# A fused retention and hard-swish kernel: one group of attention work per block instead of two

## The chip, the cores and the metric

The kernel runs on one core of one Trainium2 chip. The metric is the device time of one execution in microseconds; the time before is the median of three runs. A profile of one further execution shows what each engine did: TensorE (PE, its weight loads PEld), VectorE (DVE), ScalarE (ACT), GpSimd (POOL) and SyncE (SP).

## The reference

Eight batches of eight heads with 576 positions of 64 numbers go through a retention layer; its output goes through a two-layer network with a hard swish.

```python
scores = q @ k^T / 8                       # [B, H, 576, 576]
ret = scores * gamma_h ** (i - j)          # where i >= j, else 0
x = (ret @ v), heads side by side          # [4608, 512]
h = x @ w_in                               # [4608, 2048]
g = h * clip(h + 3, 0, 6) / 6
out = g @ w_out                            # [4608, 512]
```

## The kernel before

**Pieces and blocks.** The 576 positions of a batch are cut into four pieces of 128 and a rest of 64; the rests of two batches form a piece. This makes 36 pieces. Four pieces fill one block of 512 tokens, so there are nine blocks, 0 to 8. The last block holds the rests.

**Retention of one piece.** A piece's output is the old state of its batch times its queries (`inter`, L361), plus masked scores times values (`intra`, L377). Scores are taken from transposed keys and queries: `scores` (L343) writes a PSUM tile of two banks, tag "sc", and gives back a mask that VectorE applies from PSUM; `scores_second` (L765) writes two banks, ScalarE copies them to a tile "raw", and its mask works from there. `update_mm` (L394) computes the new part of the state, `update_state` (L411) adds and scales it on VectorE, and `spread_state` (L427) copies it on ScalarE into a block-diagonal matrix for the next `inter`. The output is cast into the token block `xt` by ScalarE (`Output.cast`, L261).

**The network of one block.** The first layer, `gemm1` (L900), has 16 units of four 512-column matmuls; each unit's hard swish takes one ScalarE and one VectorE instruction (L449, L450). From block 1 on the second layer is done with seven products instead of eight, in the manner of Strassen and Winograd: four sums of quarters of the hidden block (`sum_of`, L514, on VectorE), seven `product`s of 16 matmuls each (L529), and a `gather` (L555) behind each. Product 6 reads sum 2, product 5 sum 1, product 7 sum 3, product 3 sum 4. Products 1, 6, 7, 4 accumulate in one bank "b", product 2 in "a", and 5, 3 in "c".

**Order around the change.** The order of all instructions on each engine is written out by hand. `seven_block` (L800) does the second layer of block kb, and among its products the retention of the four pieces c0 to c3 of block kb+1; it also starts the scores of the first two pieces, n0 and n1, of the block after that. For blocks 2 to 7 it goes so: sums 1 and 2 (and, ahead of and behind them, the scaling and DMA transposes of n0 and n1, `ahead`, L755), updates of states c2-4 and c3-4, products 1, 2, 6, a group for c0 and c1 (inter, intra, update, then scores of c2 and c3), sum 3, mask, sum 4, product 5, mask, products 7 and 3, a group for c2 and c3 (with the scores of n0 and n1), masks, product 4. Then comes the first layer of block kb+1, in which n2 and n3 are scaled and transposed, at units 1 and 5.

**Buffers.** PSUM has eight banks: four of tag "ph", two of "sc", one "o", one "tu". Keys ("kn") and queries with values ("qv") have six buffers each; POOL issues their loads (`load`, L106, three DMAs per full piece) in the order of the pieces, and each waits until its buffer is free: that of "kn" is free when `update_mm` has read it, that of "qv" when the scaled copy is made (`transpose_q`, L337). SP issues the DMA transposes and the stores of the outputs (`store2`, L620), in that order of the program.

Of the kernel before, what the change touches and what calls it, by code (L numbers as in the profile page):

```python
# [10 lines left out]
FP32 = mybir.dt.float32  # L11
FP16 = mybir.dt.float16
# [5 lines left out]
def kernel(  # L18
# [64 lines left out]
    def xt_of(kb):  # L83

        if kb not in xts:
            if kb == B:
                xts[kb] = big.tile([P, NCC, MBLK], FP16, name="xt_rest")
            else:
                xts[kb] = xpool.tile([P, NCC, MBLK], FP16, tag="xt", name=f"xt_{kb}")
        return xts[kb]  # L90
# [2 lines left out]
    EARLY = 4  # L93
    SEVEN = 1
    NBUF = 6

    def by_twos(b, s0):

# [6 lines left out]

    def load(c, parts="kqv"):  # L106
        if c not in loaded:
            kn = nat.tile([P, H, D], FP16, tag="kn", bufs=NBUF, name=f"kn_{c}")
            qv = nat.tile([P, 2, H, D], FP16, tag="qv", bufs=NBUF, name=f"qv_{c}")
            loaded[c] = {"kn": kn, "qv": qv, "q16": qv[:, 0]}  # L110
            if c < EARLY:
                loaded[c]["q2"] = q2_tile(c)
        to = {"k": (loaded[c]["kn"], k), "q": (loaded[c]["qv"][:, 0], q),
              "v": (loaded[c]["qv"][:, 1], v)}
        for dst, src in (to[part] for part in parts):
            for p0, b, s0, n in pieces[c][3]:
                if src is q and c < EARLY:
                    nc.gpsimd.dma_start(loaded[c]["q2"], by_twos(b, s0))
                    continue
                nc.gpsimd.dma_start(dst[p0:p0 + n],  # L120
                                    src[b, :, s0:s0 + n, :].rearrange("h s d -> s h d"))
# [6 lines left out]
    def load_wout(c0, c1):  # L128
# [9 lines left out]
    k0 = work.tile([P, H, D], FP32, tag="osb", bufs=4, name="whole_k_0")  # L138
    nc.sync.dma_start(k0, k[0, :, 0:P, :].rearrange("h s d -> s h d"))
    v0 = work.tile([P, H, D], FP32, tag="osb", bufs=4, name="whole_v_0")  # L140
    loaded[0] = {"kn": nat.tile([P, H, D], FP16, tag="kn", bufs=NBUF, name="kn_0"),
                 "q2": q2_tile(0), "v": v0}
    nc.gpsimd.dma_start(loaded[0]["q2"], by_twos(0, 0))
    zeros = const.tile([P, MBLK], FP16)
# [31 lines left out]

    nc.vector.memset(v0[:, 0, 0:1], 0.0)
    nc.sync.dma_start(v0, v[0, :, 0:P, :].rearrange("h s d -> s h d"))
    d2 = const.tile([HALF, 2 * H, HALF], FP16)
    nc.vector.tensor_tensor(  # L180
        out=d2, in0=ident16[0:HALF, None, 0:HALF].to_broadcast([HALF, 2 * H, HALF]),
        in1=g2q.rearrange("g t h -> g (t h)")[:, :, None].to_broadcast([HALF, 2 * H, HALF]),
# [58 lines left out]
    class Output:  # L241
# [16 lines left out]
        def pair(self, p, r=slice(0, P), cols=slice(0, P)):  # L258
            return self.banks[p // self.n][r, p % self.n, cols]

        def cast(self, xt, g0):  # L261
            engines = (nc.scalar.copy, nc.vector.tensor_copy)
            for i, bank in enumerate(self.banks):
                engines[i](xt[:, i * self.n:(i + 1) * self.n, g0:g0 + P], bank)  # L264

# [111 lines left out]
    def intra(c, copy_later=False, more=False):  # L377
        o, at, vs = st[c]["o"], st[c]["at"], st[c]["vs"]
        for p in range(NPAIR):
            for h2 in range(2):  # L380
                r = slice(h2 * HALF, h2 * HALF + HALF)
                nc.tensor.matmul(o.pair(p, r), vs[:, 2 * p + h2, :], at[:, h2, p, :],  # L382
                                 start=(st[c]["first"] and o.begins(p)),
                                 stop=(o.ends(p) and not more), skip_group_check=True)
        kb, g0 = place_of(c)

        def copy():
            o.cast(xt_of(kb), g0)

        if copy_later:  # L390
            return copy
        copy()

    def update_mm(cs):  # L394

        cs = [c for c in cs if pieces[c][0] != "rest"]
        if not cs:
            return
        u = psum.tile([P, len(cs), NPAIR, D], FP32, tag="tu", name=f"u_{cs[0]}")
        for j, c in enumerate(cs):  # L400
            kn, vs = loaded[c]["kn"], st[c]["vs"]
            st[c]["u"] = u[:, j]
            for p in range(NPAIR):
                for h2 in range(2):
                    r = slice(h2 * HALF, h2 * HALF + HALF)
                    nc.tensor.matmul(u[r, j, p, :], kn[:, 2 * p + h2, :], vs[:, 2 * p + h2, :],  # L406
                                     start=(j == 0 and p == 0),
                                     stop=(j == len(cs) - 1 and p == NPAIR - 1),
                                     skip_group_check=True)

    def update_state(c):  # L411
        kind, b, i, _ = pieces[c]
        if kind == "rest":
            return
        u = st[c]["u"]
        scale = gc_b[1 if i == PER - 1 and b % 2 else 0]
        tag, bufs = ("tf", B) if i == PER - 1 else ("ts", 2 * GROUP)
        ts = work.tile([P, NPAIR, D], FP16, tag=tag, bufs=bufs, name=f"ts_{c}")
        if i == 0:
            nc.vector.tensor_tensor(out=ts, in0=u, in1=scale, op=ALU.mult)  # L420
        else:
            ta = work.tile([P, NPAIR, D], FP32, tag="ta", bufs=2, name=f"ta_{c}")
            nc.vector.tensor_tensor(out=ta, in0=u, in1=state_of[b], op=ALU.add)
            nc.vector.tensor_tensor(out=ts, in0=ta, in1=scale, op=ALU.mult)
        state_of[b] = ts

    def spread_state(c, copy=nc.scalar.copy):  # L427

        kind, b, i, _ = pieces[c]
        if kind == "rest" or i == PER - 1:  # L430
            return
        ts, bd = state_of[b], spare.pop(0)
        spare.append(bd)
        st.setdefault(c + GROUP, {})["before"] = bd
        copy(bd[0:HALF, :, 0:D], ts[0:HALF])
        copy(bd[HALF:P, :, D:2 * D], ts[HALF:P])
# [273 lines left out]
    def load_until(c):  # L710
        while next_load[0] < NP and next_load[0] <= c:
            load(next_load[0])
            next_load[0] += 1
# [41 lines left out]
    def ahead(c):  # L755
        transpose_k(c)
        transpose_q(c)

    def load_behind(c, c1):

        turn = work.tile([P, 1], FP16, tag="turn", bufs=1, name="turn")
        nc.gpsimd.tensor_copy(turn, st[c]["vs"][:, 0, 0:1])
        load_until(c1)
# [36 lines left out]
    def seven_block(kb, mine, next_):  # L800

        seven[kb] = {}
        c0, c1, c2, c3 = mine
        n0, n1, n2, n3 = next_ or [None] * 4

        def both(which):
            for tt in range(2):
                product(kb, which, tt)

        def begin(one, other, tags):  # L810
            masks[one] = scores(one, given=True)
            masks[other] = scores_second(other, tags)

        def mask(c):
            masks.pop(c)()

        def done(*cs):
            for c in cs:
                loaded.pop(c)

        run_later(9)
        if kb > SEVEN and next_:
            ahead(n0)
        for i, q1 in done_to[kb].items():
            sum_of(kb, i, q1, 8)
        if kb == SEVEN:
            begin(c0, c1, ("ph", "ph"))
        else:
            if next_:
                ahead(n1)  # L830
            update_state(c2 - GROUP)
            update_state(c3 - GROUP)
        both(1)
        gather(kb, 1)
        spread_state((c2 if kb == SEVEN else c0) - GROUP)
        if kb == SEVEN:
            mask(c0)
            mask(c1)
            ahead(n0)
        both(2)  # L840
        gather(kb, 2)
        spread_state((c3 if kb == SEVEN else c1) - GROUP)
        if kb == SEVEN:
            sum_of(kb, 3, 0, 8)
            ahead(n1)
            load_behind(n1, c1 + NBUF)
        both(6)
        gather(kb, 6)
        if kb == SEVEN:
            both(5)  # L850
            gather(kb, 5)
            sum_of(kb, 4, 0, 8)
        inter(c0, "ph" if kb == SEVEN else "o")
        inter(c1, "ph")
        intra(c0)
        intra(c1)
        update_mm([c0, c1])
        begin(c2, c3, ("ph", "ph"))
        done(c0, c1)
        load_until(c3 + NBUF)  # L860
        if kb == SEVEN:
            mask(c2)
        else:
            sum_of(kb, 3, 0, 8)
            mask(c2)
            sum_of(kb, 4, 0, 8)
            both(5)
            gather(kb, 5)
        mask(c3)
        update_state(c0)  # L870
        if kb > SEVEN:
            spread_state(c2 - GROUP)
        both(7)
        gather(kb, 7)
        update_state(c1)
        if kb > SEVEN:
            spread_state(c3 - GROUP)
        both(3)
        gather(kb, 3)
        inter(c2, "ph")  # L880
        inter(c3, "ph")
        intra(c2)
        intra(c3)
        update_mm([c2, c3])
        done(c2, c3)
        if next_:
            begin(n0, n1, ("ph", "o"))
            load_until(n1 + NBUF)
            mask(n0)
            mask(n1)  # L890
        both(4)
        gather(kb, 4)

# [104 lines left out]
```

## Time and profile before

| What | us |
|---|---|
| median of three runs (lowest, highest) | 292.73 (292.62, 293.09) |
| the profiled execution's own time | 292.64 |
| its span, first to last instruction | 290.9 |
| block 5: product 1 to the end of product 4 | 184.86 to 200.98, 16.1 |
| block 5: first layer of block 6 behind it | 200.98 to 214.80, 13.8 |
| VectorE busy in the span | 236.8 |

Times inside the profile count from the span's start. A line of a timeline has start, length, engine, line, operation, tiles and shapes. In the chain of what ended last, a piece's length ends where its last matmul ends, while the matmuls themselves overlap: each is issued before the one ahead has left the array. A tile's name stands left of the arrow, what it is made from right of it. "DMA to landing" is the time from issue to the last byte.

### The profile page before, as it was taken

Reading aid. Unit: us, or ns where it says so; the run is one execution under the profiler, and the core shown is the slowest. Engines: PE = TensorE matmul, PEld = TensorE weight load, DVE = VectorE, ACT = ScalarE, POOL = GpSimd, SP = SyncE. Lnnn points to the kernel's source line nnn. Section 1 sums busy time; section 2 is a strip of 40 time slices with the busy share of each in tenths; the row PEclk is TensorE's granted clock in tenths of the full one; section 3 lists DMA queues with packets and bytes.
Section 4 is the critical chain, followed back from the end, with each engine's and each line's share of the span. In section 5 each row is a group of like instructions: output and inputs, shape, how many; then the busy total and the mean of one; then the engine's idle time right before and its main releaser. Section 6 shows DMA issues by size and latency. Waiting matters only on the chain.

```text
span 290.9 us, 6752 instructions
## 1 busy us (share of the span) xinstructions
PE 283.9 (98%) x2708; PEld 185.5 (64%) x2708; DVE 236.8 (81%) x410; ACT 181.4 (62%) x312; POOL 107.1 (37%) x134
## 2 busy tenths in 40 slices
PE   7999999999999999999999999999999999999993
PEld 3554456548854786478647864687468745874582
DVE  7689659999979996998699859995999599818951
ACT  6568436785477657744786668765876586437711
POOL 8953669510870077007700770067443200000000
PEclk9999999999999999999999999999999999999999
DMA  9999999999999499919992999199989960021014
GB/s 132 165 202 201 191 156 215 170 151 107 102 201 172 71 101 223 151 30 98 209 163 44 85 205 169 39 84 194 183 58 94 129 130 3 2 78 70 1 38 108
DMA packets 151807, 35.83 MB, mean 123 GB/s; under 512 B 141536, under 2 KB 147680, under 8 KB 151776
## 3 DMA queue, kind: packets, MB, share of 16 engines
q0 software_dynamic: 113664, 18.10, 89.2%
q1 hardware_dynamic: 37808, 17.05, 30.8%
q8 instruction: 21, 0.34, 0.6%
q10 hardware_dynamic: 304, 0.26, 0.3%
q14 instruction: 10, 0.08, 0.1%
HBM read 36.70 MB, written 9.44 MB: 159 GB/s over the span
## 4 chain that ended last, share of the span: by engine, by line
PE 94%; DMA 2%; DVE 1%; issue 1%; ACTq 0%; ACT 0%; POOL 0%; POOLq 0%
PE ph L442 41%; PE b L551 19%; PE c L551 10%; PE pout L492 5%; PE a L551 5%; PE o L382 4%; PE sc L350 2%; PE o L270 2%; PE ph L465 2%; DMA kn<-in_k_dram 2%; PE u L406 1%; PE sc L773 1%; PE warm L222 1%; DVE at L354 1%; PE trk L304 1%
## 5 line engine op out<-in xcount | busy, mean ns | idle before, releaser
L449 ACT ACTIVATE u<-ph,cb 128x512 f32<-128x512 f32 x144 | 98.6, 690 | 25.3 <-PE ph L442 23.0
L450 DVE SCALAR_TENSOR_TENSOR gt<-u,ph 128x512 f16<-128x512 f32 x144 | 95.8, 685 | 20.9 <-ACT u L449 18.6
L442 PE MATMUL ph<-xt,win 128*128 128x512 f16 x488 | 106.6, 379 | 0.0
L442 PEld LDWEIGHTS <-win 128*128 128x128 f16 x552 | 54.0, 98 | 63.2
L120 POOL DMA_DIRECT2D kn<-in_k_dram x39 | 33.3, 858 | 94.5 <-PE u L406 76.4
L551 PEld LDWEIGHTS <-s 128*128 128x128 f16 x512 | 49.4, 98 | 6.6 <-DVE s L525 0.2
L551 PEld LDWEIGHTS <-gt 128*128 128x128 f16 x384 | 36.3, 98 | 7.4 <-DVE gt L450 1.1
L120 POOL DMA_DIRECT2D qv<-in_v_dram x39 | 33.8, 874 | 2.8 <-DMA wout<-in_moe_w_out_dram 1.7
L120 POOL DMA_DIRECT2D qv<-in_q_dram x36 | 30.8, 862 | 5.3 <-DMA wout<-in_moe_w_out_dram 3.3
L354 DVE TENSOR_TENSOR at<-sc,mask_wide 128x1024 f16<-128x1024 f32 x19 | 23.2, 1223 | 9.5 <-PE sc L350 9.5
L551 PE MATMUL b<-tw,s 128*128 128x256 f16 x256 | 30.6, 273 | 0.0
L264 ACT CAST xt<-o 128x512 f16<-128x512 f32 (+1 forms) x32 | 17.2, 577 | 19.2 <-PE o L382 17.2
L525 DVE TENSOR_TENSOR s<-gt 128x512 f16<-128x512 f16 (+1 forms) x37 | 22.7, 614 | 0.1
L561 ACT COPY part<-b 128x512 f32<-128x512 f32 x14 | 8.2, 587 | 20.1 <-PE b L551 20.1
L340 DVE TENSOR_TENSOR vs<-qv,gqv 128x1024 f16<-128x1024 f16 x28 | 19.2, 685 | 0.0
L551 PE MATMUL b<-wout,gt 128*128 128x256 f16 x128 | 15.7, 273 | 0.0
L551 PE MATMUL b<-tw,gt 128*128 128x256 f16 x128 | 15.4, 273 | 0.0
L551 PE MATMUL c<-tw,s 128*128 128x256 f16 x128 | 15.3, 273 | 0.0
L551 PE MATMUL a<-wout,gt 128*128 128x256 f16 x128 | 15.3, 273 | 0.0
L551 PE MATMUL c<-wout,s 128*128 128x256 f16 x128 | 15.3, 272 | 0.0
L779 ACT CAST raw<-sc 128x512 f16<-128x512 f32 x28 | 15.1, 594 | 0.0
L492 PE MATMUL pout<-wout,gt 128*128 128x512 f16 x64 | 14.8, 379 | 0.0
(97 smaller groups left out, 276.6 us busy)
## 6 DMA issues: line engine op xcount, KB each, us to landing
kn<-in_k_dram POOLq DMA_DIRECT2D x31, 128.0 KB, 5.7
qv<-in_v_dram POOLq DMA_DIRECT2D x31, 128.0 KB, 6.7
qv<-in_q_dram POOLq DMA_DIRECT2D x28, 128.0 KB, 6.2
out_dram<-olo SPq DMA_DIRECT2D x7, 512.0 KB, 4.8
out_dram<-ohi SPq DMA_DIRECT2D x7, 512.0 KB, 4.9
wout<-in_moe_w_out_dram POOLq DMA_DIRECT2D x4, 512.0 KB, 14.8
win<-in_moe_w_in_dram POOLq DMA_DIRECT2D x4, 256.0 KB, 7.0
win<-in_moe_w_in_dram POOLq DMA_DIRECT2D x2, 512.0 KB, 10.6
```

The source lines that it names most:

```text
L120: nc.gpsimd.dma_start(dst[p0:p0 + n], src[b, :, s0:s0 + n, :].rearrange("h s d -> s h d"))
L264: engines[i](xt[:, i * self.n:(i + 1) * self.n, g0:g0 + P], bank)
L340: nc.vector.tensor_tensor(out=vs, in0=loaded[c]["qv"], in1=gqv, op=ALU.mult)
L354: mask = lambda: nc.vector.tensor_tensor(out=at.rearrange("t a b s -> t (a b) s"), in0=sc.rearrange("t a b s -> t (a b) s"), in1=mask_b[pi ...
L382: nc.tensor.matmul(o.pair(p, r), vs[:, 2 * p + h2, :], at[:, h2, p, :], start=(st[c]["first"] and o.begins(p)), stop=(o.ends(p) and not mo ...
L442: nc.tensor.matmul(ph, win16[:, dmc, P * fc:P * fc + P], xt_of(kb)[:, dmc, :], start=(dmc == 0), stop=(dmc == NCC - 1))
L449: nc.scalar.activation(u, ph, ACTF.Relu, bias=cb[:, 0:1], scale=1.0 / 6.0)
L450: nc.vector.scalar_tensor_tensor(out=gts[kb][:, fc, :], in0=u, scalar=1.0, in1=ph, op0=ALU.min, op1=ALU.mult)
L492: nc.tensor.matmul(pout, gt[:, fc, P * mc:P * mc + P], wout16[:, fc, :], start=(fc == 0), stop=(fc == NFC - 1))
L525: nc.vector.tensor_tensor(out=sm[i][:, q], in0=one, in1=other, op=op)
L551: nc.tensor.matmul(my[chain][tt], left[:, k, P * tt:P * tt + P], right[:, k, :], start=(first and (tt == 0 or apart) and k == 0), stop=(k ...
L779: nc.scalar.copy(raw[:, h2], banks[h2])
```

## The change

Block 1 keeps its order in a function of its own, `first_seven`. In blocks 2 to 7 `seven_block` now goes: sums 1 and 2 and the two state updates as before, product 1, scores of c2 and c3 with the mask of c2, spreading of c0 and c1's states, product 2, sum 3, mask of c3, product 6, sum 4, spreading of c2 and c3's states, products 5, 7, 3, and then one group: `inter` of all four pieces, `intra` of all four, updates of all four, scores of n0 and n1, the updates of states c0 and c1, the masks of n0 and n1, product 4. The outputs of the first three pieces lie in "ph" banks, that of the fourth in half of "sc", from which VectorE casts it. The updates of c2 and c3 lie in bank "o". All four loads of the later block are asked for behind the group. The keys have eight buffers; the table `d2`, used for the first four pieces' queries only, moves into a buffer that outputs use later.

```diff
+    KBUF = 8
...
-            kn = nat.tile([P, H, D], FP16, tag="kn", bufs=NBUF, name=f"kn_{c}")
+            kn = nat.tile([P, H, D], FP16, tag="kn", bufs=KBUF, name=f"kn_{c}")
...
-    d2 = const.tile([HALF, 2 * H, HALF], FP16)
+    d2 = work.tile([HALF, 2 * H, HALF], FP16, tag="osb", bufs=4, name="d2")
...
         if kb == SEVEN:
-            begin(c0, c1, ("ph", "ph"))
...
+            first_seven(kb, mine, next_, both, begin, mask, done)
+            return
+        if next_:
+            ahead(n1)
+        update_state(c2 - GROUP)
+        update_state(c3 - GROUP)
         both(1)
         gather(kb, 1)
...
+        begin(c2, c3, ("ph", "ph"))
+        mask(c2)
+        spread_state(c0 - GROUP)
+        spread_state(c1 - GROUP)
         both(2)
         gather(kb, 2)
...
+        sum_of(kb, 3, 0, 8)
+        mask(c3)
         both(6)
         gather(kb, 6)
...
+        sum_of(kb, 4, 0, 8)
+        spread_state(c2 - GROUP)
+        spread_state(c3 - GROUP)
+        both(5)
+        gather(kb, 5)
+        both(7)
+        gather(kb, 7)
+        both(3)
+        gather(kb, 3)
+        for c, tag in zip(mine, ("ph", "ph", "ph", "sc")):
+            inter(c, tag)
+        for c in mine[:3]:
+            intra(c)
+        intra(c3, copy_later=True)((nc.vector.tensor_copy,))
+        update_mm([c0, c1])
+        update_mm([c2, c3], "o")
+        done(*mine)
+        if next_:
+            begin(n0, n1, ("ph", "ph"))
+            load_until(n3 + GROUP)
+        update_state(c0)
+        update_state(c1)
+        if next_:
+            mask(n0)
+            mask(n1)
+        both(4)
+        gather(kb, 4)
```

More of the change, by code (lines that the diff above doesn't have):

```diff
@@ L140 @@
     v0 = work.tile([P, H, D], FP32, tag="osb", bufs=4, name="whole_v_0")
-    loaded[0] = {"kn": nat.tile([P, H, D], FP16, tag="kn", bufs=NBUF, name="kn_0"),
+    loaded[0] = {"kn": nat.tile([P, H, D], FP16, tag="kn", bufs=KBUF, name="kn_0"),
                  "q2": q2_tile(0), "v": v0}
@@ L259, in pair, with cast @@
             return self.banks[p // self.n][r, p % self.n, cols]
-        def cast(self, xt, g0):
-            engines = (nc.scalar.copy, nc.vector.tensor_copy)
+        def cast(self, xt, g0, engines=(nc.scalar.copy, nc.vector.tensor_copy)):
             for i, bank in enumerate(self.banks):
@@ L385, in intra, with copy @@
         kb, g0 = place_of(c)
-        def copy():
-            o.cast(xt_of(kb), g0)
+        def copy(*engines):
+            o.cast(xt_of(kb), g0, *engines)
         if copy_later:
@@ L392, in intra, with update_mm @@
         copy()
-    def update_mm(cs):
+    def update_mm(cs, tag="tu"):
         cs = [c for c in cs if pieces[c][0] != "rest"]
@@ L398, in update_mm @@
             return
-        u = psum.tile([P, len(cs), NPAIR, D], FP32, tag="tu", name=f"u_{cs[0]}")
+        u = psum.tile([P, len(cs), NPAIR, D], FP32, tag=tag, name=f"u_{cs[0]}")
         for j, c in enumerate(cs):
@@ L826, in seven_block @@
         if kb == SEVEN:
-            begin(c0, c1, ("ph", "ph"))
[L828 to L832, printed above, removed]
+            first_seven(kb, mine, next_, both, begin, mask, done)
[4 more added lines that the diff above has]
+        update_state(c3 - GROUP)
         both(1)
         gather(kb, 1)
-        spread_state((c2 if kb == SEVEN else c0) - GROUP)
@@ L836, in seven_block @@
[L836 to L839, printed above, removed]
+        begin(c2, c3, ("ph", "ph"))
+        mask(c2)
+        spread_state(c0 - GROUP)
+        spread_state(c1 - GROUP)
         both(2)
         gather(kb, 2)
[L842 to L846, printed above, removed]
+        sum_of(kb, 3, 0, 8)
+        mask(c3)
         both(6)
         gather(kb, 6)
[L849 to L852, printed above, removed]
@@ L853, in seven_block @@
-        inter(c0, "ph" if kb == SEVEN else "o")
+        sum_of(kb, 4, 0, 8)
[14 more added lines that the diff above has]
+        update_mm([c2, c3], "o")
@@ new lines, in seven_block, with first_seven @@
+        done(*mine)
[9 more added lines that the diff above has]
+        gather(kb, 4)
+    def first_seven(kb, mine, next_, both, begin, mask, done):
+        c0, c1, c2, c3 = mine
+        n0, n1, n2, n3 = next_
+        begin(c0, c1, ("ph", "ph"))
+        both(1)
+        gather(kb, 1)
+        spread_state(c2 - GROUP)
+        mask(c0)
+        mask(c1)
+        ahead(n0)
+        both(2)
+        gather(kb, 2)
+        spread_state(c3 - GROUP)
+        sum_of(kb, 3, 0, 8)
+        ahead(n1)
+        load_behind(n1, c1 + NBUF)
+        both(6)
+        gather(kb, 6)
+        both(5)
+        gather(kb, 5)
+        sum_of(kb, 4, 0, 8)
+        inter(c0, "ph")
@@ L860, in seven_block @@
         load_until(c3 + NBUF)
[L861 to L868, printed above, removed]
+        mask(c2)
         mask(c3)
         update_state(c0)
-        if kb > SEVEN:
-            spread_state(c2 - GROUP)
         both(7)
@@ L875, in seven_block @@
         update_state(c1)
-        if kb > SEVEN:
-            spread_state(c3 - GROUP)
         both(3)
@@ L885, in seven_block @@
         done(c2, c3)
[L886 to L890, printed above, removed]
+        begin(n0, n1, ("ph", "o"))
+        load_until(n1 + NBUF)
+        mask(n0)
+        mask(n1)
         both(4)
```

## The prediction, as it was made before the result

> **What bounds the kernel now.** I read the page first (busy shares, chain), then the table of waits, then the chain and the timelines of one block, and the DMA views last. The page's first part and the first line of its chain:
>
> ```profile
> PE 283.9 (98%) x2708; PEld 185.5 (64%) x2708; DVE 236.8 (81%) x410; ACT 181.4 (62%) x312; POOL 107.1 (37%) x134
> PE 94%; DMA 2%; DVE 1%; issue 1%; ACTq 0%; ACT 0%; POOL 0%; POOLq 0%
> ```
>
> TensorE is busy almost always and carries 94% of the chain. In the table of waits no matmul of blocks 2 to 7 stands with a wait worth naming; other engines wait for TensorE. A busy share doesn't say that the matmuls run at their pace, so I looked at the chain of block 5 (start, length, what; in us):
>
> ```profile
> 184.86 1.80 PE b L551 x16
> 186.66 1.75 PE a L551 x16
> 188.40 1.75 PE b L551 x16
> 190.15 0.45 PE o L270 x8
> 190.60 0.57 PE o L382 x16
> 191.16 0.25 PE u L406 x16
> 191.41 0.33 PE sc L350 x8
> 191.74 0.22 PE sc L773 x8
> 191.97 1.85 PE c L551 x16
> ```
>
> These are products 1, 2, 6, the first group (old state, attention, update, two scores), and product 5. A product takes 1.75 wherever it follows a product: no hole. So TensorE has nothing to win except what it loses between its own kinds of work: the product behind the scores takes 1.85, 0.10 more; the first scores take 0.33 and the second 0.22, 0.11 more; 16 attention matmuls take 0.57, where an early group of 8 takes 0.34, so 8 cost 0.23, 16 would cost 0.46, and 0.11 is the entry. **The next engine in line is VectorE**, 81% busy, and inside a block it is nearly full. Its timeline there:
>
> ```profile
> 189.28 0.42 DVE L423 TENSOR_TENSOR ta<-u,ts 128x256 f32<-128x256 f32 x1
> 189.73 0.43 DVE L424 TENSOR_TENSOR ts<-ta,gc 128x256 f16<-128x256 f32 x1
> 190.07 0.68 DVE L564 TENSOR_TENSOR olo<-part,a 128x512 f32<-128x512 f32 x1
> 190.67 1.22 DVE L525 TENSOR_TENSOR s<-gt 128x2048 f16<-128x2048 f16 x1
> 191.81 1.22 DVE L354 TENSOR_TENSOR at<-sc,mask_wide 128x1024 f16<-128x1024 f32 x1
> 192.94 1.22 DVE L525 TENSOR_TENSOR s<-gt,s 128x2048 f16<-128x2048 f16 x1
> 194.07 0.69 DVE L782 TENSOR_TENSOR at<-raw,mask_wide 128x1024 f16<-128x1024 f16 x1
> ```
>
> Each starts before the one ahead of it ends, so an instruction costs its step from start to start: 0.60 for gather 2 (L564), 1.14 for sum 3, 1.13 for the mask from PSUM, about 0.60 for the mask from SBUF. VectorE runs without a break from 184 to 196. It isn't late only because the first group keeps TensorE away from product 7 (the reader of sum 3) for 1.8 us.
>
> **The change, part by part.**
>
> *Tile shapes.* The numbers of matmuls stay. Instead of two entries into attention there is one: 0.11 saved per block. The scores of the third and fourth piece now follow a product directly, which the trace doesn't show; bounds are no entry at all (0) and twice the dearest entry (0.2). I take the 0.11 of scores behind updates, the nearest row, and the 0.10 of a product behind scores stays. Saved: 0.11 in each of six blocks, 0.66.
>
> *Scores and masks ahead of sum 3.* In the old order VectorE did gather 2, then sum 3, then the first mask. Now mask 3 (128x1024 from PSUM) stands ahead of both. VectorE comes free at 190.07, since all ahead of that (two scalings, the rest of sums 1 and 2, two state updates) is as before. Mask 190.07 to 191.20, gather 2 to 191.80, sum 3 starts 191.80 and ends 1.22 later, 193.02; a matmul starts some 0.05 after the VectorE result that it awaits: 193.07. TensorE meanwhile: the timeline starts product 2's first matmul at 186.49, 0.17 before the chain's boundary, as a matmul ends later than it issues. Behind product 1 come the entry and two scores (0.65 to product 2's start), so product 2 starts at 187.14, and products 6, 5, 7 at 188.90, 190.65 and 192.40. Product 7 waits 193.07 - 192.40 = **0.67**. Queued behind it on TensorE is everything else of the block; nothing later gives it back, since all of it is the chain. Sum 4 then ends at 194.76 (mask 4 from 192.94, 0.60; sum 4 from 193.54, 1.22) and product 3 would start at 194.82: just in time.
>
> Who pays: blocks 2, 3, 5 and 6 have the same distance from product 2's boundary to VectorE's gather 2 (3.42 us in each). Block 4 updates the states of first pieces, one instruction each instead of two:
>
> ```profile
> 158.54 0.75 DVE L420 TENSOR_TENSOR ts<-u,gc 128x256 f16<-128x256 f32 x2
> 159.21 0.68 DVE L564 TENSOR_TENSOR olo<-part,a 128x512 f32<-128x512 f32 x1
> ```
>
> There product 2's boundary is 156.72, 2.49 before VectorE's 159.21; it is 0.9 earlier, and product 7 has 0.25 to spare. Block 7 has no next block to scale for (two scalings of 0.60 less), so it doesn't wait either. Four blocks: 4 x 0.67 = 2.68.
>
> *Fourth output in the scores' bank.* The next scores need the bank out of which VectorE casts the fourth output. Between lie 32 update matmuls, 0.50. The cast starts 0.04 after the last attention matmul ends. VectorE's cast of 128x512 from PSUM isn't in the trace. Rows around it:
>
> ```profile
> L264 DVE CAST xt<-o x2: 424/424/425, 17.2 to 52.7; 128x256 f16<-128x256 f32 x2
> ```
>
> Half the size takes 0.42; the mask of twice the size 1.22; additions of 128x512 out of PSUM 0.69. I take 0.69, the same size and source. The bank is free 0.04 + 0.69 + 0.05 = 0.78 after attention's end; the scores could start 0.50 - 0.07 = 0.43 after it (0.07 is how far their first matmul starts ahead of the chain's boundary, 191.35 against 191.41). Wait **0.35**; by the ends of the cast, 0.08 to 0.88. The Trainium skill, "PSUM — Partial Sum Buffer", section on bank collisions, asks that no two engines touch one bank and quadrant at once; the trace has no such overlap. By that rule the wait can't be softened by writing another column. Blocks 2 to 6 pay, block 7 has no next scores: 5 x 0.35 = 1.75.
>
> *What stays hidden.* VectorE behind the group, from the last attention matmul's issue: cast to 0.86, two updates to 2.46, two masks to 4.20; the next first layer's first use of VectorE comes at 5.03 (scores at 1.00, product 4 at 1.55, first layer at 3.40, its first VectorE instruction 1.63 later, as 142.73 against 141.10). Spare 0.8; with that cover gone, each 0.1 costs 0.1. ScalarE's casts of outputs one to three (0.59 each) end one by one during attention, so two of the four "ph" banks are free for the second scores. Raw casts, parts (0.59 each) and eight spreading copies (0.42 each) make 6.3 us of ScalarE work beside five products and the scores, over 9 us; its last item, the copy of product 5, ends at about 193.7, and product 3 needs it at 194.8. Product 5's bank "o" is free when the second state update has read it, at 189.70; needed 190.65. The moved table for the early queries costs nothing: its buffer's next user comes after 40 us.
>
> *Loads.* POOL issues 12 loads in one run behind the group, 0.87 each, 10.4 us, instead of six and six. SP's order of transposes and stores is the old one, only the first store goes some 3 us earlier. Block 4's last transpose for the third and fourth piece landed 12.2 us after the first layer's start; it is now needed at about 15.9. Six more loads may cost up to 6 x 0.87 = 5.2, but the earlier store leaves that stretch; I count nothing. In block 1 the eight key buffers let the loads of pieces 18 and 19 go at about 85 instead of 102.7, onto a busy DMA. The last transpose for piece 15 there:
>
> ```profile
> qk<-vs SPq DMA_TRANSPOSE x1, 7.0
> ```
>
> issued at 89.45, it lands at 96.46 and is now needed at 97.94: 1.5 to spare. While loads were still landing it got through, so I take it as hidden.
>
> **Sum.** -0.66 + 2.68 + 1.75 = +3.77 on the profiled execution's 292.64 (its span of 290.9 and 1.7 around it): 296.4. The runs' median is 292.73, 0.09 above that execution; I make no correction.
>
> **Rivals.**
> *Transposes come late* (299.5). If the six added loads of block 1 are served ahead of piece 15's transpose, it lands 5.2 later, 101.7, 3.7 after its need, of which product 7's 0.67 in block 2 would have been lost anyway: +3.1. For it: DMA is full there, and a transpose alone takes a fraction of 7 us. Against: transposes land between loads in the trace. The Trainium skill, "DMA: Bandwidth & Descriptors", section on queues, rings and completion order, says that a DMA engine goes round the queues packet by packet; by it a longer load queue doesn't lengthen the turn, and the time stays that of the forecast. The trace agrees so far: a transpose issued at 85.92 landed at 94.98, ahead of a load issued at 84.61 (96.24). Chance 0.13.
> *One wait only.* VectorE half a microsecond earlier at sum 3 than I count: 292.64 + 1.75 - 0.66 = 293.7; a cast as fast as the small one: 295.0. Chance 0.12.
> *Not slower: entries between tile shapes are dearer than the rows say.* Place: the one entry less per block. Its price would have to be (2.68 + 1.75)/6 = 0.74 us to pay for both waits (292.6); from there on the change is no loss, and at 0.84 a gain of 0.6. The rows say 0.10 to 0.11. Or VectorE is late nowhere: 292.0. Together 0.10.
> Forecast 0.60; other losses, larger than these, 0.05.
>
> The range takes in the bounds of the unknown costs: 296.4 less 1.35 for the quick cast and 0.66 for no entry, 294.4, to 296.4 with 2.65 for the slow cast and 0.54 for the dear entry, 299.6; late transposes are inside. A measurement can tell about 0.2% from no change. Faster by more than that 0.05, within it 0.05, slower 0.90.
>
> **What would show it.** In the changed profile: product 7 of blocks 2, 3, 5, 6 waiting about 0.67 for VectorE's sum 3, and not in blocks 4 and 7; the scores behind the group waiting 0.35 for VectorE's cast; products at 1.75 otherwise; no matmul waiting for a transpose. I am wrong if product 7 doesn't wait, if scores of the third or fourth piece wait for a DMA, or if first-layer matmuls wait for banks.

## The result and the profile after

The changed kernel takes 296.71 us (median of four runs, 296.38 to 297.01) beside 292.68 of the kernel before (four runs, one more than in the table above): a ratio of 1.0136, 95% interval 1.0118 to 1.0154. It is slower by 4.0 us. The profiled execution took 296.49, 3.85 more than the one before, and its span grew from 290.9 to 294.7.

The first part of the page and the first line of its chain, for the changed kernel:

```profile
PE 284.1 (96%) x2708; PEld 184.9 (63%) x2708; DVE 239.2 (81%) x416; ACT 178.2 (60%) x306; POOL 107.0 (36%) x134
PE 21%; DVE 1%; ACTq 0%; ACT 0%; issue 0%
```

TensorE's busy time is what it was (283.9 before) with the same number of matmuls, so the whole difference is idle time between them. The chain's shares don't add up to the span, since it could be followed back only to 224 us; they aren't to be set against the 94% of before.

The table of waits for TensorE alone, from 90 us to the last blocks (who, for whom, us in total, times, longest):

```profile
PE sc L350 <- DVE xt L264: 1.4, 5, 0.3
PE sc L773 <- DMA qk<-vs: 1.3, 2, 0.7
PE b L551 <- DVE s L525: 1.0, 2, 0.5
```

Before, nothing stood here. Now there are three kinds of wait: scores behind the group for the cast of the fourth output (five times), scores of the fourth piece for a DMA transpose (twice), product 7 for sum 3 (twice). The second kind in TensorE's timeline, in block 2 (in brackets the idle time before the matmul and what ended it):

```profile
97.61 0.40 PE L350 MATMUL sc<-qk 64*128 64x128 f16 x8
98.69 0.40 PE L773 MATMUL sc<-qk 64*128 64x128 f16 x8 [0.69 <-DMA qk<-vs]
```

The idle time of this view begins at the modelled end of the matmul before, so it is shorter than what the start of the waiting matmul loses: 0.5 here is 0.67 of delay.

Two of the three in the chain of block 6 (start, length, what):

```profile
224.47 0.59 DVE olo L564
225.06 1.15 DVE s L525
226.21 0.04 issue
226.25 1.92 PE b L551 x16
228.17 1.75 PE c L551 x16
229.92 0.89 PE o L270 x16
230.81 1.03 PE o L382 x32
231.85 0.02 issue
231.87 0.70 DVE xt L264
232.57 0.04 issue
232.62 0.40 PE sc L350 x8
```

The chain leaves TensorE twice: for gather 2 and sum 3 on VectorE ahead of product 7 (PE b), and for the 0.70 us cast (DVE xt L264) ahead of the next scores. The updates, 0.50 us, lie beside the cast and are no longer in the chain. And VectorE's timeline in block 5:

```profile
192.39 1.22 DVE L354 TENSOR_TENSOR at<-sc,mask_wide 128x1024 f16<-128x1024 f32 x1
193.52 0.68 DVE L564 TENSOR_TENSOR olo<-part,a 128x512 f32<-128x512 f32 x1
194.11 1.22 DVE L525 TENSOR_TENSOR s<-gt 128x2048 f16<-128x2048 f16 x1
195.25 0.69 DVE L782 TENSOR_TENSOR at<-raw,mask_wide 128x1024 f16<-128x1024 f16 x1
195.86 1.22 DVE L525 TENSOR_TENSOR s<-gt,s 128x2048 f16<-128x2048 f16 x1
```

The mask now runs ahead of gather 2 and sum 3; sum 3 ends at 195.33 and product 7's first matmul starts at 195.39.

From the last first-layer matmul of a block to the first of the next, the trace gives (us):

| Block | before | after | difference | waits of TensorE there |
|---|---|---|---|---|
| 2 | 16.34 | 17.44 | +1.10 | transpose, cast |
| 3 | 15.45 | 16.48 | +1.03 | transpose, cast |
| 4 | 16.34 | 16.58 | +0.24 | cast |
| 5 | 16.34 | 17.27 | +0.93 | sum 3, cast |
| 6 | 16.34 | 17.27 | +0.93 | sum 3, cast |
| 7 | 15.64 | 15.40 | -0.24 | none |

The sum is +3.99; all else agrees within 0.2. Told by when the waiting matmuls start, the delays are 0.85 and 0.79 for the two transposes and twice 0.67 for product 7.

### The profile page after: what moved, and what is told of

It reads as the page before. It is cut to its first block, busy times and chain, and to the rows that moved or that the text cites. A ratio compares the mean times of both kernels' runs of the same rounds, so it can differ in the third digit from the quotient of the medians.

```text
span 294.7 us, 6754 instructions
## 1 busy us (share of the span) xinstructions
PE 284.1 (96%) x2708; PEld 184.9 (63%) x2708; DVE 239.2 (81%) x416; ACT 178.2 (60%) x306; POOL 107.0 (36%) x134
## 5 line engine op out<-in xcount | busy, mean ns | idle before, releaser
L450 DVE SCALAR_TENSOR_TENSOR gt<-u,ph 128x512 f16<-128x512 f32 x144 | 95.9, 683 | 16.7 <-ACT u L449 14.4
L121 POOL DMA_DIRECT2D kn<-in_k_dram x39 | 33.9, 875 | 83.0 <-PE u L406 76.8
L264 ACT CAST xt<-o 128x512 f16<-128x512 f32 (+1 forms) x27 | 14.2, 575 | 26.2 <-PE o L382 24.1
L551 PE MATMUL a<-wout,gt 128*128 128x256 f16 x128 | 15.3, 273 | 0.0
L551 PE MATMUL c<-tw,s 128*128 128x256 f16 x128 | 15.3, 273 | 0.0
L551 PE MATMUL c<-wout,s 128*128 128x256 f16 x128 | 15.3, 273 | 0.0
```

The source lines that it names most:

```text
L121: nc.gpsimd.dma_start(dst[p0:p0 + n], src[b, :, s0:s0 + n, :].rearrange("h s d -> s h d"))
L450: nc.vector.scalar_tensor_tensor(out=gts[kb][:, fc, :], in0=u, scalar=1.0, in1=ph, op0=ALU.min, op1=ALU.mult)
L551: nc.tensor.matmul(my[chain][tt], left[:, k, P * tt:P * tt + P], right[:, k, :], start=(first and (tt == 0 or apart) and k == 0), stop=(k ...
```

## The experiments

My theory: three waits, each with a cause of its own. VectorE's order makes products 7 and 3 wait; the place of the fourth output makes the next scores wait; the loads in one run make the fourth piece's transpose late, and where they do, that delay hides product 7's. The main rival: the load run slows the block as a whole, and the waits are its symptoms. The diffs are against the changed kernel, except the last. Beside the first four of these kernels the kernel before takes 292.97, beside the others 292.86, so a time is best read as its distance from that; the changed kernel's was 4.03.

### Sum 3 ahead of the masks

```diff
-        mask(c2)
         spread_state(c0 - GROUP)
...
         sum_of(kb, 3, 0, 8)
+        mask(c2)
         mask(c3)
```

> The changed kernel, with sum 3 on VectorE ahead of the masks of the third and fourth piece; sum 4 stays behind both masks. Theory A (VectorE has too much to do before products 7 and 3, whatever its order): in blocks 5 and 6 product 7 no longer waits, but sum 4 still ends when it did, so product 3 waits instead, about 0.66 us; time as the changed kernel, 296.7. Theory B (only the place of the one mask costs): the 0.67 us in blocks 5 and 6 vanish and no wait takes their place, 295.4. In both the scores behind the group wait 0.35 us in five blocks and the scores of the fourth piece wait for a transpose in blocks 2 and 3, 0.8 us each, as in the changed kernel.

Measured: 296.94, ratio 1.0135 (1.0118 to 1.0152), 3.97 above the kernel before and so as the changed kernel. The waits of TensorE in block 6:

```profile
PE c L551 <- DVE s L525: 0.5, 1, 0.5
PE sc L350 <- DVE xt L264: 0.3, 1, 0.3
```

The waiting product is now one of bank "c", product 3, and its wait is as long as product 7's was. Theory A holds: VectorE has 0.67 us too much to do ahead of the last of the two sums. Theory A named block 5 too; in this execution a late transpose took the place of that wait there (0.69 of delay), and of half of it in block 3 (0.36, with 0.31 left for product 3).

### Both sums ahead of both masks

```diff
         sum_of(kb, 3, 0, 8)
-        mask(c3)
         both(6)
         gather(kb, 6)
         sum_of(kb, 4, 0, 8)
+        mask(c2)
+        mask(c3)
```

(The mask of c2 ahead of the spreading is gone too.)

> The changed kernel, with sums 3 and 4 both ahead of the two masks. Theory A (VectorE's order around the sums is what products wait for): no product waits in blocks 5 and 6, 2 x 0.67 less, 295.4; blocks 2 and 3 keep their wait for a transpose, which had hidden this one, so nothing is gained there. Theory B (the loads in one run slow the whole block, VectorE and transposes alike): the product waits move but the time stays at 296.7.

Measured: 295.38, ratio 1.0082 (1.0067 to 1.0097), 2.41 above the kernel before. No matmul waits for a sum any more, and block 6, where no transpose is late in either kernel, is 0.24 longer than in the kernel before instead of 0.93. The rival, by which the time would stay, falls. That the expected 295.4 came out is in part luck. In the profiled execution TensorE idled for a transpose in blocks 2 (0.88) and 5 (0.45) and not in block 3: block 5, which was to gain 0.67, gained 0.07, and block 3, which was to gain nothing, gained 0.8. So which blocks pay for late transposes differs between executions. Up to the wait in block 2 this kernel, those of the experiments on sum 3, on the fourth piece and on two repairs, and the changed kernel run the same program; yet in their five executions the transpose lands 16.4 to 17.3 after the first layer's start, and TensorE loses 0.55 to 1.42 there.

### The fourth piece's attention first

```diff
+        intra(c3, copy_later=True)((nc.vector.tensor_copy,))
         for c in mine[:3]:
             intra(c)
-        intra(c3, copy_later=True)((nc.vector.tensor_copy,))
```

> The changed kernel, with the fourth piece's attention first in the group and the other three behind it, so that VectorE's cast out of the scores' bank has 0.7 us more. Theory A (the scores wait for this cast alone): the 0.35 us in blocks 2 to 6 vanish, 1.7 less, 295.0. Theory B (the wait is then taken over by the second scores, which need the banks of the first two outputs, cast later by ScalarE): a wait of up to 0.3 us stays, 296 to 296.7.

Measured: 295.72, ratio 1.0113 (1.0065 to 1.0161; one of its four runs took 298.45, so the interval is wide, and no trace shows why), 2.75 above the kernel before. No scores wait for the cast any more: block 4 goes from +0.24 to -0.07 beside the kernel before, blocks 5 and 6 from +0.93 to +0.62, so the wait was worth 0.31. Over the six blocks of the profiled execution the gain is 1.1 and not 5 x 0.31: in block 2 TensorE idled 1.25 for the transpose instead of 0.69, which ate the gain there, and in block 3 product 7's wait took the place of the transpose's. Theory B falls: the second scores wait for no cast.

### The loads spread

```diff
             ahead(n1)
+            load_behind(n1, n3)
...
-            load_until(n3 + GROUP)
+            load_until(n1 + GROUP)
...
-        load_until(n1 + NBUF)
+        load_until(n1 + GROUP)
```

The last edit is in `first_seven`; `load_behind` holds POOL back until the second piece is scaled.

> The changed kernel, with the loads spread again: two pieces behind each group, the other two behind the scaling of the second piece at the next block's start, in block 1 too. Theory A (the longer load run makes the fourth piece's transpose late in blocks 2 and 3, and this wait hides product 7's): the waits for transposes, 0.8 us each, vanish, and product 7 of blocks 2 and 3 waits 0.67 for VectorE as in blocks 5 and 6; together 0.2 less, 296.5. Theory B (the load run costs the whole difference): about 293. Theory C (the transposes are late for another reason): unchanged, with the same waits for transposes.

Measured: 296.37, ratio 1.0117 (1.0102 to 1.0132), 3.40 above the kernel before. The waits of TensorE:

```profile
PE b L551 <- DVE s L525: 2.1, 4, 0.5
PE sc L350 <- DVE xt L264: 1.4, 5, 0.3
```

The transposes are in time everywhere, and product 7 waits in four blocks instead of two: blocks 2, 3, 5 and 6 are all 0.93 longer than before. One wait had stood in front of another. This is theory A: the six blocks together are 0.25 shorter than in the changed kernel, where 0.2 was expected, and the load run costs little as long as product 7 waits anyway. The distance between the medians shrank by more, 0.6; the ratios' intervals overlap, so this difference isn't clear of noise.

### Two repairs, then three

The first kernel has the two edits of "Both sums ahead of both masks" and "The fourth piece's attention first" together:

```diff
         sum_of(kb, 4, 0, 8)
+        mask(c2)
+        mask(c3)
...
+        intra(c3, copy_later=True)((nc.vector.tensor_copy,))
         for c in mine[:3]:
             intra(c)
```

> The changed kernel, with both sums ahead of both masks and the fourth piece's attention first in its group, the loads still in one run. Theory A (three separate waits that add up): the product waits and the waits for the cast are gone, 1.35 and 1.7 less than 296.7, so 293.7; what stays is the wait for the fourth piece's transpose in blocks 2 and 3, and in some runs in block 5, 0.8 to 1.7 us in all. Theory B (the late transposes come from TensorE's other waits and go with them): 292.2.

Measured over ten runs: 293.58 (293.25 to 294.57), ratio 1.0028 (1.0017 to 1.0039). Only waits for a transpose are left in the profiled execution, 0.4 in block 2 and delays of 0.1 at most in blocks 4 and 5. With the loads spread as well:

> The changed kernel with all three repairs: both sums ahead of both masks, the fourth piece's attention first, the loads spread. Theory A: no matmul of blocks 2 to 7 waits; each of blocks 2 to 6 is 0.11 shorter than in the kernel before and block 7 is 0.24 shorter, 0.8 in all: 292.1 beside 292.9 on this chip, a ratio of 0.997. Theory B (without the waits the new order still costs something, as a further wait that the others hid): 293.5 or more.

Measured: 292.11 beside 292.86, ratio 0.9968 (0.9956 to 0.9981), faster than the kernel before by 0.3%. With product 7's wait and the cast's gone, spreading the loads is worth 1.5 us between the medians; alone it had brought little. In the trace no matmul of blocks 2 to 7 waits. Its chain in block 5, behind product 3:

```profile
196.28 0.89 PE o L270 x16
197.18 1.01 PE o L382 x32
198.19 0.50 PE u L406 x32
198.70 0.33 PE sc L350 x8
199.03 0.27 PE sc L773 x8
199.29 1.85 PE b L551 x16
```

The group runs through without a hole, and the updates are back in the chain. Blocks 2 to 6 are 0.07 to 0.08 shorter than in the kernel before, block 7 is 0.24 shorter. So without its waits the new grouping is worth 0.6 us in the blocks' lengths, 0.75 between the medians.

### The buffers alone, in the kernel before

```diff
+    KBUF = 8
...
-    d2 = const.tile([HALF, 2 * H, HALF], FP16)
+    d2 = work.tile([HALF, 2 * H, HALF], FP16, tag="osb", bufs=4, name="d2")
```

(and the eight buffers where the keys' tiles are made).

> The kernel before, with only the eight key buffers and the moved table of the change, its order of work unchanged. Theory A: no wait of TensorE comes of it; the loads of two pieces go earlier in every block and transposes land later, but scores of the third and fourth piece stand late enough: 292.9, as before. Theory B (earlier loads by themselves make transposes late enough to stop TensorE): 294 or more, with scores waiting for a transpose.

Measured: ratio 0.9999 (0.9990 to 1.0008), no block differs by more than 0.01. Yet the last transpose of piece 15 lands 16.6 us after its first layer's start, as late as in the changed kernel (16.8; in the kernel before 14.5). The late landing costs something only because the new order asks for it at 15.9. So block 2's late transpose comes from the eight key buffers, which let further loads go earlier in block 1, and not from the loads in one run, of which my theory made one cause for both blocks. In block 3 it is the run: with the buffers alone the same transpose lands at 11.8, in the changed kernel at 16.7. The experiment with spread loads undid both, since it changed block 1 too.

## Why the prediction was right, and where it was not

The forecast was 296.4, the measurement 296.7. Two of the three waits were foreseen with cause and size, the cast's in all its five blocks and product 7's in two of its four; the third, for transposes, was counted at nothing, and scores of the fourth piece waiting for a DMA stood in the prediction's own list of signs that it is wrong. By its steps:

- **VectorE ahead of product 7.** Right in place and size in blocks 5 and 6 (195.39 against a due start of 194.72: 0.67), right that block 4 is spared and that the time doesn't come back. In blocks 2 and 3 the wait didn't occur, because TensorE had already lost that time to a transpose; the run with spread loads shows that it was there behind it. "Sum 4 just in time" was right too: the chain shows product 3 following product 7 at once.
- **The cast out of the scores' bank.** Right: five times, cast 0.70 against the assumed 0.69, worth 0.31 against 0.35 (the scores do start 0.35 later, and the steps behind them give 0.03 back).
- **The entries.** Counted at 0.66, 0.11 in each of six blocks; with the waits gone they are 0.07 to 0.08 in each of five blocks and 0.24 in block 7, together 0.61. Attention took twice 0.57 in block 5 and takes 1.01, so one entry less saves 0.13; but the second scores behind the group take 0.27 where they took 0.22, and why is open. Block 7 has no such scores, and its old states, matmuls of another shape (L276), save an entry as well, twice 0.62 against 1.13. The forecast had neither the dearer second scores nor this second entry, and the totals agree by luck. That scores directly behind a product pay 0.11 was right: the first take 0.33, the second 0.22, as behind updates.
- **The loads.** This step failed, in both of its parts. For the longer run it says "I count nothing", and for block 1's earlier loads "I take it as hidden". In blocks 2 and 3 the fourth piece's scores start 0.8 us late, both times for its transpose. For block 2 the forecast kept the old landing, 96.46, with 1.5 to spare; it was 98.65. The rival that named this gave it to block 2 alone, 3.7 late. Two answers of the DMA view for the last transpose of the fourth piece in block 3's first layer, first the kernel before, then the changed one:

```profile
qk<-vs SPq DMA_TRANSPOSE x1, 3.8
```

```profile
qk<-vs SPq DMA_TRANSPOSE x1, 9.2
```

From issue to landing 3.8 and 9.2 us. Before, the loads of that stretch had landed 10.3 us after the first layer's start, and the last transposes, undisturbed, landed 0.4 to 0.6 apart. Now loads go on landing until 18.7, and transposes come 1.4 to 2.9 apart: 10.7, 13.6, 15.3, 16.7. My working asked whether transposes can overtake loads. They do, so the rule of the Trainium skill that I set beside it ("DMA: Bandwidth & Descriptors", queues, rings and completion order) isn't contradicted. But it answers for the turn, not for how long turns must be shared: the last of the old transposes landed when no load was left to share with.

That the sum came out right although a step failed is luck, and the runs show how it came about: in blocks 2 and 3 the late transpose (0.8) and product 7's wait (0.67) lie one behind the other, so that only the longer one shows, and the two happen to be of nearly one size. Twice 0.8 - 0.67 is 0.3 us more than forecast, the smaller wait for the cast takes 0.2 back, and the profiled execution is 3.85 longer where 3.77 was forecast.

Not tried: how late the transposes would be with loads in still smaller runs. In blocks 3 to 5 of the five kernels that keep the changed kernel's loads, the last transpose of the fourth piece lands 15.2 to 16.7 after the first layer's start, while its scores are due at 15.9 (in the changed kernel's blocks 4 and 5 it lands at 15.88 and 15.90). So a few tenths decide which block pays; what moves the landing from one execution to another stays open.

## What to carry to other kernels

Where one engine runs without a hole, moving its work costs whatever the other engines can't have ready at the new time: write down, for each operand of each moved step, when it is ready and when it will be wanted. A wait found this way may stand in front of another, so removing one alone can bring little or nothing (spread loads, sum 3 alone); the repairs must be tried together before the order is judged. A DMA's landing in the old trace holds only with the old traffic around it: if a burst is made longer, see which transfers landed early because the burst had ended.

## What the runs showed of the hardware

In the first layers of blocks 2 to 5 a DMA transpose of 128 KB issued from SP, which was issued well before the one ahead of it had landed, came 0.2 to 0.6 us behind that one where no load was left (kernel before), and 1.0 to 2.9 us behind it while POOL's loads were under way (changed kernel). The landing of block 2's last such transpose moved by 0.9 us between executions of one order of work. VectorE's cast of 128x512 out of PSUM to half precision takes 0.69 to 0.70 us, as long as an addition of that size, while ScalarE's takes 0.59.
